# All steps of an attention and feed-forward kernel in another order: what moves when the first V chunk is loaded early and small clears and copies change engine

## The chip, the cores and the metric

The kernel runs on one core of a Trainium2 chip. The metric is the device time of the program in microseconds (us), as the median of timed runs. In the names of the profile PE is the matrix engine (TensorE) and PEld its weight load, DVE is VectorE, ACT is ScalarE, POOL is GpSimd, and SP is the engine that only issues transfers; POOL issues the loads that convert 32 bit floats to 16 bit on the way.

## The reference

Windowed attention (8 global keys, 96 local ones, a bias that falls with distance) and a SwiGLU block behind it. All is given as 32 bit floats.

```python
# q, k, v: (4, 8, 768, 64); w_gate, w_val: (512, 1536); w_out: (1536, 512)
scores = q @ k.transpose(0, 1, 3, 2) / sqrt(64)
keep   = is_global | is_local            # key < 8, or 0 <= query - key < 96
scores = where(keep, scores - slope[h] * dist, -1e9)
a      = softmax(scores, axis=-1)
x      = (a @ v).transpose(0, 2, 1, 3).reshape(3072, 512)
out    = (silu(x @ w_gate) * (x @ w_val)) @ w_out     # (3072, 512)
```

## The kernel before

**Tiles.** A batch of the attention has 768 tokens in two halves of 384. Keys stand in 7 chunks of 120, each with the 8 global keys copied in front, so that a chunk fills 128 rows. Heads go in pairs (0 to 3), pairs in two groups g (0: pairs 0 and 1; 1: pairs 2 and 3). The feed-forward block takes the tokens in 8 tiles t of 384: tile 2b + half is one half of batch b. All weights are kept on chip in 16 bit; the products write to 8 banks of the accumulator memory, which are dealt out in the order of the steps: a product that needs a bank waits until the instruction that read the bank's last contents has run.

**The order.** There is no loop over batches. The string ORDER lists 1035 steps, and the loop at L772 to L774 calls one function for each. Each engine runs its instructions in the order in which the steps issue them and waits only for data, buffers and banks. So ORDER is five queues in one: PE, VectorE, ACT, POOL (mostly loads) and SP (transposes by DMA, stores, small loads). A step that waits holds up all that stands behind it on its engine.

The steps that the text names, with their numbers as arguments:

| step | what it does | engine | line |
|---|---|---|---|
| Lf, Li, Ld | first rows of batch 0; identity; masks' distances (Ld.S.2 is the early mask) | SP, ACT, POOL | L280, L267, L274, L276 |
| Lh.i.half.h0.h1 | half of batch 0's keys (i = 0) or queries (i = 1), four heads | POOL | L284 |
| Lv.b.c | chunk c of batch b's V | POOL | L292 |
| Lw, Lo | parts of gate and value weights (256 KB); thirds of the output weights (512 KB) | POOL | L351, L356 |
| L4, Lr.b.i.h | rows of four heads of batch 1; rows of one head (96 KB) | POOL | L333, L344 |
| Z.b.engine | clears the unused rows of batch b's V buffer, two memsets | by the letter | L309 |
| G.b.c0.c1.engine | copies the 8 global V rows to chunks c0 to c1 - 1 | by the letter | L303, L305 |
| X.b.r...engine | copies V across to the other half of the rows (vX) | by the letter | L319 |
| cast, T, k, q | casts, transposes and places batch 0's keys and queries; k also copies the global keys, always on VectorE (L436) | A or V, PE | L400, L417, L430, L446 |
| b, C, E, V | batch 0's first half: bias, scores, exponentials, weighting of V | PE, ACT | L549, L564, L573, L586 |
| U, kw, qw | batch 1, pairs 0 and 1: transposes on PE, placing | PE, A or V | L455, L463, L473 |
| D.b.pair.i, K.b.pair | the other pairs and batches: transposes by DMA from the rows that Lr loaded; K places keys | SP, VectorE | L483, L490 |
| c, x, m, B | scores, exponentials, masks (M makes them), bias | PE, ACT, VectorE | L520, L530, L539, L504 |
| w, i, j, r, p, W | sums, their inverses, copies beside, spreading, weighting of V (W), scaling (p) | PE, VectorE, ACT | L630, L647, L659, L663, L614, L678 |
| g, t, s, v, h | gate product, tanh, silu, value product, hidden, for tile t and one of 12 columns f | PE, ACT, VectorE | L693, L699, L703, L709 |
| o.t.i.part, e | output product, a quarter each; scaling and store | PE, ACT, SP | L734, L752 |

**Buffers.** V of a batch (vS, tag "vS") has two buffers, dealt in the order of the steps that first use them. Batch 0 and batch 1 take them first. In the order before, batch 3 (Z.3) takes batch 0's and batch 2 (Z.2) takes batch 1's. The staged rows of a batch (stage, tags "kst" and "qst") have two buffers each in the same way. The eight loads that POOL has in flight have one semaphore each, so that the ninth waits for the first to land.

**The order around the change.** The first FFN product is g.0.0; ahead of it stand batch 0's first half and the scores of its second half. From then on PE has FFN products of earlier tiles to do while a batch is prepared. The first product of batch 1 is g.2.1, behind the scaling of its first half (p.1.1.0.1).

Of the kernel before, what the change touches and what calls it, by code (L numbers as in the profile page):

```python
# [84 lines left out]
Z.3.P s.1.10 U.0.1 U.1.1 U.0.0 t.1.0 s.1.0 t.1.1 g.1.11 kw.1.V kw.0.A v.1.10 v.1.1 qw.0.A Lv.1.6
qw.1.A g.1.2 g.1.8 g.1.3 t.1.11 s.1.1 s.1.11 t.1.8 v.1.0 t.1.3 t.1.2 h.1.10 h.1.1 M.1.0 s.1.3 v.1.2
g.0.6 h.1.0 v.1.11 s.1.8 g.1.9 s.1.2 Lv.1.1 M.0.0 g.1.6 h.1.2 Lw.1.1.1 h.1.3 t.1.9 g.0.5 s.1.9
Lr.2.1.3 h.1.11 c.1.0.0.0 t.0.6 t.0.5 t.1.6 s.0.6 c.1.0.0.1 x.1.0.0.1 D.1.2.1 v.1.8 Lv.1.5 g.1.4
s.1.6 g.0.7 g.0.4 h.1.8 s.0.5 v.1.9 v.0.6 Lr.2.0.4 Lv.1.0 t.0.7 x.1.0.0.0 s.0.7 M.3.0 h.1.9 K.1.3
Lo.0 Lo.1 g.1.7 t.0.4 v.1.6 c.1.0.1.0 h.0.6 t.1.7 s.0.4 s.1.7 v.0.7 Lo.2 Lr.2.0.0 h.1.6 v.1.4 Lv.1.2  # L90
h.0.7 v.1.7 t.1.4 g.1.5 v.0.4 Lv.1.4 s.1.4 v.0.5 Lv.1.3 h.1.7 t.1.5 v.1.5 K.1.2 h.1.4 h.0.4 Lr.2.0.3
h.0.5 c.1.1.1.1 Lr.2.1.2 c.1.1.0.0 x.1.0.1.0 c.1.1.0.1 s.1.5 h.1.5 M.2.1 o.0.1.0 o.0.2.0 x.1.1.1.1
x.1.1.0.1 o.0.0.0 Lr.2.0.7 M.2.0 m.1.1.1.1.V o.1.2.0 Lr.2.1.5 Lr.2.1.4 G.1.1.7.S Lr.3.1.2 o.0.0.1
m.1.0.0.0.V Lr.2.0.6 o.1.2.1 x.1.1.0.0 c.1.0.1.1 c.1.1.1.0 o.0.2.1 o.0.0.2 x.1.1.1.0 o.0.1.1 o.1.2.2
o.1.2.3 m.1.1.0.1.V o.0.2.2 m.1.1.0.0.V x.1.0.1.1 m.1.0.0.1.V m.1.1.1.0.V m.1.0.1.1.V m.1.0.1.0.V
w.1.0 X.1.1.0.7.V w.1.1 o.0.1.2 X.1.0.0.7.A i.1.0 i.1.1 o.0.0.3 j.1.0.A r.1.0.0.1 o.0.1.3 W.1.0.1
# [713 lines left out]
```

## Time and profile before

| | before |
|---|---|
| timed runs (us) | 235.59, 237.2, 237.91; median 237.2 |
| span of the profiled execution, first to last instruction (us) | 235.1 |
| time of the profiled execution apart from its span | not given; its DMA packets end at 233.7 us |
| PE busy | 228.1 us, 97% |
| DVE busy | 166.8 us, 71% |
| ACT busy | 117.0 us, 50% |
| POOL busy | 79.1 us, 34%, up to 116 us |
| granted TensorE clock | 1.000 |
| loads and stores | 25.97 MB, 110 GB/s over the span |

How to read it: the profile is of one execution. Times in it are us from the span's start. A busy PE is not a PE at its peak, since its products are pipelined and their ends are modelled. Brackets behind an instruction of the timeline give the engine's idle time ahead of it and what ended it. The view of windows gives for each engine the busy time in a stretch, with the instructions in brackets, then the clock, the DMA share and GB/s.

### The profile page before, as it was taken

What the parts mean: (1) busy time and instruction counts of PE and PEld (TensorE: products, weight loads), DVE (VectorE), ACT (ScalarE), POOL (GpSimd) and SP (SyncE); (2) the same over time, 40 slices, a digit from 0 to 9 for tenths busy, and PEclk for the clock granted to TensorE, in tenths of its full rate; (3) what the DMA queues carried; (4) which work ended last, traced back from release to release, by engine and by line L of the source; (5) the groups of instructions that cost most, each with busy time, mean ns of one, the idle gap of its engine ahead of it and who ended that gap; (6) DMA issues with size and microseconds to landing.
All of it is one profiled execution on the core that took longest, in us unless ns stands there. A gap on an engine that the chain in (4) does not pass through costs nothing.

```text
span 235.1 us, 6093 instructions
## 1 busy us (share of the span) xinstructions
PE 228.1 (97%) x2504; PEld 132.2 (56%) x2504; DVE 166.8 (71%) x385; ACT 117.0 (50%) x220; POOL 79.1 (34%) x113
## 2 busy tenths in 40 slices
PE   7889999998899999999999999999999999999997
PEld 5556556555455656655555565556655565554444
DVE  2698996888549798877798998979776467461020
ACT  4679736783546703827826687744231334140421
POOL 8985778664264079787700000000000000000000
DMA  6999999999999999999999610200000120000323
GB/s 170 190 179 205 203 189 185 130 137 146 202 149 163 204 163 136 110 144 138 146 179 197 68 47 3 89 3 0 3 0 0 45 92 1 0 25 22 134 91 134
DMA packets 88324, 25.97 MB, mean 110 GB/s; under 512 B 78048, under 2 KB 85256, under 8 KB 88296
## 3 DMA queue, kind: packets, MB, share of 16 engines
q0 software_dynamic: 67120, 14.25, 78.7%
q1 hardware_dynamic: 20488, 10.74, 24.5%
q10 hardware_dynamic: 688, 0.59, 0.7%
q8 instruction: 19, 0.31, 0.6%
q14 instruction: 9, 0.07, 0.1%
HBM read 28.93 MB, written 6.29 MB: 150 GB/s over the span
## 4 chain that ended last, share of the span: by engine, by line
PE 65%; DMA 23%; POOL 6%; DVE 3%; issue 1%; ACT 0%; SPq 0%; DVEq 0%; POOLq 0%; ACTq 0%
PE banks L693 39%; PE banks L734 20%; DMA vS<-in_v_dram 6%; DMA kst<-in_k_dram 5%; DMA wv<-in_moe_w_val_dram 4%; DMA qst<-in_q_dram 4%; DMA k<-in_k_dram 3%; PE banks L614 2%; PE banks L520 2%; POOL vS L292 1%; DMA out_dram<-osb 1%; PE banks L723 1%; POOL qst L344 1%; POOL q L284 1%; PE banks L630 1%
## 5 line engine op out<-in xcount | busy, mean ns | idle before, releaser
L699 ACT ACTIVATE th<-banks 128x384 f32<-128x384 f32 x96 | 43.9, 493 | 68.1 <-PE banks L693 66.5
L693 PE MATMUL banks<-xT,wv 128*128 128x384 f16 x384 | 71.7, 326 | 0.4 <-DMA wv<-in_moe_w_val_dram 0.3
L693 PE MATMUL banks<-xT,wg 128*128 128x384 f16 x384 | 70.6, 326 | 0.0
L709 DVE TENSOR_TENSOR hT<-banks,sl 128x384 f16<-128x384 f32 x96 | 50.9, 551 | 22.8 <-PE banks L693 19.8
L734 PE MATMUL banks<-wo,hT 128*128 128x512 f16 x276 | 65.3, 379 | 0.6 <-DMA wo<-in_moe_w_out_dram 0.6
L703 DVE SCALAR_TENSOR_TENSOR sl<-th,banks 128x384 f32<-128x384 f32 x96 | 50.2, 546 | 19.3 <-ACT th L699 18.8
L693 PEld LDWEIGHTS <-wv 128*128 128x128 f16 x384 | 36.8, 98 | 26.3 <-DMA wv<-in_moe_w_val_dram 0.7
L693 PEld LDWEIGHTS <-wg 128*128 128x128 f16 x384 | 37.2, 98 | 25.5 <-DVE xT L678 0.2
L734 PEld LDWEIGHTS <-hT 128*128 128x128 f16 x276 | 26.3, 98 | 29.2 <-DMA wo<-in_moe_w_out_dram 0.8
L530 ACT ACTIVATE at<-banks 128x1008 f16<-128x1008 f32 (+3 forms) x28 | 25.7, 957 | 10.6 <-PE banks L520 9.6
L292 POOL DMA_DIRECT2D vS<-in_v_dram x28 | 25.1, 906 | 5.9 <-DMA qst<-in_q_dram 3.0
L752 ACT ACTIVATE osb<-banks 128x512 f32<-128x512 f32 x23 | 13.5, 597 | 20.0 <-PE banks L734 16.5
L539 DVE TENSOR_TENSOR at<-at,masks 128x1008 f16<-128x1008 f16 (+3 forms) x26 | 16.2, 645 | 5.3 <-ACT at L530 4.9
L344 POOL DMA_DIRECT2D qst<-in_q_dram x20 | 16.8, 843 | 8.4 <-DMA wo<-in_moe_w_out_dram 5.2
L344 POOL DMA_DIRECT2D kst<-in_k_dram x20 | 16.7, 839 | 5.5 <-DMA wo<-in_moe_w_out_dram 2.0
L663 DVE STREAM_TRANSPOSE rb<-dR 128x384 f32<-128x384 f32 x32 | 17.1, 555 | 0.1
L678 DVE TENSOR_TENSOR xT<-banks,rb 128x384 f16<-128x384 f32 x22 | 11.0, 542 | 1.0 <-PE banks L614 0.8
L319 ACT COPY vX<-vS 64x1792 f16<-64x1792 f16 (+2 forms) x7 | 9.0, 1287 | 3.3 <-DMA vS<-in_v_dram 3.1
L520 PEld LDWEIGHTS <-kT 64*64 64x64 f16 x456 | 7.4, 107 | 5.5 <-issue 5.1
L520 PE MATMUL banks<-qT,kT 64*64 64x152 f16 (+9 forms) x456 | 9.1, 214 | 0.9 <-DMA qT<-qst 0.7
L614 PE MATMUL banks<-at,vS 64*64 64x152 f16 (+9 forms) x228 | 8.0, 213 | 0.4 <-DVE hT L709 0.4
L614 PEld LDWEIGHTS <-vS 64*64 64x64 f16 x228 | 6.7, 107 | 2.4 <-issue 2.4
(77 smaller groups left out, 150.6 us busy)
## 6 DMA issues: line engine op xcount, KB each, us to landing
out_dram<-osb SPq DMA_DIRECT2D x23, 256.0 KB, 2.5
vS<-in_v_dram POOLq DMA_DIRECT2D x24, 120.0 KB, 8.4
kst<-in_k_dram POOLq DMA_DIRECT2D x20, 96.0 KB, 7.5
qst<-in_q_dram POOLq DMA_DIRECT2D x20, 96.0 KB, 7.2
wg<-in_moe_w_gate_dram POOLq DMA_DIRECT2D x6, 256.0 KB, 8.1
wv<-in_moe_w_val_dram POOLq DMA_DIRECT2D x6, 256.0 KB, 8.4
wo<-in_moe_w_out_dram POOLq DMA_DIRECT2D x3, 512.0 KB, 13.5
k<-in_k_dram POOLq DMA_DIRECT2D x3, 192.0 KB, 6.0
```

What stands on the lines that cost most here:

```text
L292: nc.gpsimd.dma_start(out=v_of(b)[r0:r0 + n, c, heads(g), :], in_=v[b, heads(g), KC * c:KC * c + n, :].rearrange("h p d -> p h d"))
L344: nc.gpsimd.dma_start(out=rows_of(i, b, h // 2)[:, :, h % 2, :], in_=KQ[i][b, h].rearrange("(t p) d -> p t d", p=128))
L520: nc.tensor.matmul(sc[64 * r:64 * r + 64, hi, col:col + n], lhsT=kTs[2 * g + r][d, k0:k0 + 64], rhs=qTs[b, 2 * g + r][d, q0:q0 + n], start ...
L530: nc.scalar.activation(out=at[:, :, 0:w], in_=sc[:, :, 0:w], func=AF.Exp, scale=scale)
L539: ENG[e].tensor_mul(a2, a2, masks[:, 2 * g:2 * g + 2, x:x + w])
L614: nc.tensor.matmul(num[64 * hi:64 * hi + 64, r, q0 - HB * half:q0 - HB * half + n], lhsT=vSs[b][k, c, h] if up == r else crossed[b][k, c, ...
L663: nc.vector.transpose(rb.rearrange("p (n i) -> p n i", i=32), rbs[b, half][:, g, r].unsqueeze(2).broadcast_to([128, TB // 32, 32]))
L693: nc.tensor.matmul(gv[t, f, which][:, 0:TB], lhsT=w[:, c, 128 * f:128 * f + 128], rhs=xTs[t][:, c, :], start=(c == 0), stop=(c == NC - 1))
L699: nc.scalar.activation(out=th, in_=gv[t, f, 0][:, 0:TB], func=AF.Tanh, scale=0.5)
L703: nc.vector.scalar_tensor_tensor(out=sl, in0=gv[t, f, "t"], scalar=1.0, in1=gv[t, f, 0][:, 0:TB], op0=AluOp.add, op1=AluOp.mult)
L709: nc.vector.tensor_mul(hTs[t][:, f, :], gv[t, f, 1][:, 0:TB], gv[t, f, "s"])
L734: nc.tensor.matmul(ops_t[t, i], lhsT=hTs[t][:, f, 128 * i:128 * i + 128], rhs=wo[:, f, :], start=(f == 0), stop=(f == NFF - 1))
```

## The change

Only the string ORDER changes. It has 1035 steps before and after, and all matmuls, activations and loads are the same ones, but for 19 steps that go to another engine (one of them a copy that was a DMA):

- to VectorE: the clears Z.1 and Z.2 (from POOL), the copy G.0.4.7 (from SP, where it was a DMA), k.1.1, qw.0, X.1.0, and the copies j.1.1, j.2.0, j.2.1, j.3.0 (from ACT);
- to ACT: cast.0.1, cast.1.0, q.1.1, q.3.1, k.2.1, k.3.0, X.1.1, X.2.1; cast.1.1 goes from ACT to VectorE.

The queues change as follows.

- **SP at the start:** Ld.S.2, Lf.S.0.1, Li, Lf.S.0.0 instead of Lf.S.0.1, Li, Ld.S.2, Lf.S.0.0.
- **POOL at the start:** Z.0, kz, Lh.0.0.4.8, Lh.1.0.4.8, Lh.0.1.4.8, **Lv.0.0**, Lh.1.1.0.4, Lh.0.1.0.4, Lv.0.1, Ld.P.1, Lh.1.1.4.8, Lv.0.3, Lv.0.2. Before: Z.0, Z.1, kz, Lh.0.0.4.8, Ld.P.1, Lh.1.0.4.8, Lh.1.1.4.8, Lv.0.0, Lh.0.1.0.4, Lh.1.1.0.4, Lh.0.1.4.8, Lv.0.3, Lv.0.1, Lv.0.2.
- **POOL in the middle:** ... Lr.1.1.6, Lr.1.1.7, Lw.1.1.0, **Lv.2.6**, Lo.0, Lo.1, Lv.1.0, Lo.2, Lv.1.4, Lr.2.0.5, Lv.1.3, Lv.1.6, Lv.1.2, Lv.1.1, Lv.1.5. Before: ... Lr.2.1.3, Lv.1.5, Lr.2.0.4, Lv.1.0, Lo.0, Lo.1, Lo.2, Lr.2.0.0, Lv.1.2, Lv.1.4, Lv.1.3. Lr.3.1.7, of batch 3, is now loaded ahead of batch 1's pair 3.
- **V's buffers:** batch 2 takes batch 0's, cleared by VectorE (Z.2 behind K.1.3), and batch 3 takes batch 1's, cleared by POOL.
- **PE:** the output products begin with o.1.0.0 and not with o.0.1.0; one part of o.0.1 comes behind g.2.4, now the first product of batch 1; the last products are those of tile 7, as before.

The diff, cut to the start and to the steps around Z.2, Lv.2.6 and Lo.0:

```diff
 ORDER = """
-pre Z.0.P Lf.A.1.1 Lf.S.0.1 fill.5 Z.1.P Lf.A.1.0 kz.P Li cast.0.1.V cast.1.0.V cast.1.1.A fill.10
-sl.1 Lh.0.0.4.8 sl.2 Ld.P.1 sl.0 T.1.0.0 T.1.0.1 Ld.S.2 sl.3 T.0.0.1 k.1.0.A sl.4 q.1.0.A q.0.0.V
-b.1.1 Lf.S.0.0 Lh.1.0.4.8 sl.5 sl.7 cast.0.0.V b.1.0 Lh.1.1.4.8 C.1.1 Lv.0.0 C.1.0 E.1.1 Lh.0.1.0.4
-T.0.0.0 b.2.1 b.0.0 E.1.0 k.0.0.V sl.6 b.0.1 T.2.0.0 T.3.0.0 C.0.1 k.2.0.V k.3.0.V Lh.1.1.0.4
-Lh.0.1.4.8 C.0.0 Lv.0.3 Lv.0.1 T.3.0.1 Lv.0.2 E.0.1 T.2.0.1 E.0.0 q.2.0.V G.0.4.7.S pk b.3.0
...
-s.1.6 g.0.7 g.0.4 h.1.8 s.0.5 v.1.9 v.0.6 Lr.2.0.4 Lv.1.0 t.0.7 x.1.0.0.0 s.0.7 M.3.0 h.1.9 K.1.3
-Lo.0 Lo.1 g.1.7 t.0.4 v.1.6 c.1.0.1.0 h.0.6 t.1.7 s.0.4 s.1.7 v.0.7 Lo.2 Lr.2.0.0 h.1.6 v.1.4 Lv.1.2
...
+Ld.S.2 Z.0.P kz.P Lf.S.0.1 Lf.A.1.1 Lf.A.1.0 pre Li fill.5 cast.0.1.A Lf.S.0.0 cast.1.1.V sl.3
+fill.10 sl.2 cast.0.0.V T.1.0.0 T.1.0.1 Lh.0.0.4.8 Lh.1.0.4.8 cast.1.0.A b.1.1 pk sl.6 k.1.0.A
+Lh.0.1.4.8 T.0.0.1 sl.1 Lv.0.0 Lh.1.1.0.4 T.0.0.0 b.1.0 q.1.0.A C.1.0 sl.0 C.1.1 k.0.0.V sl.7
+T.2.0.0 q.0.0.V E.1.1 sl.5 T.3.0.0 E.1.0 Lh.0.1.0.4 Lv.0.1 b.0.0 C.0.0 sl.4 b.0.1 C.0.1 T.2.0.1
+k.2.0.V E.0.0 Ld.P.1 T.3.0.1 Lh.1.1.4.8 E.0.1 b.2.1 T.2.1.0 q.2.0.V C.2.1 G.0.4.7.V w.0.0.0 q.3.0.A
+k.3.0.A b.3.1 C.3.1 b.2.0 Z.1.V k.2.1.A C.2.0 i.0.0.0 E.3.1 Lv.0.3 E.2.0 T.0.1.1 b.3.0 G.0.1.4.V
...
+K.1.3 Z.2.V x.1.0.0.0 s.0.4 g.1.7 g.1.5 h.1.9 s.1.4 t.1.7 Lv.2.6 v.1.7 t.0.6 v.0.7 v.0.6 h.1.8 v.0.4
+Lo.0 m.1.0.0.0.V M.2.0 Lo.1 h.1.6 Lv.1.0 s.1.7 t.1.5 g.0.5 M.2.1 t.0.5 s.0.6 Lo.2 h.1.7 K.1.2 v.1.4
...
+x.1.1.1.1 s.0.7 h.0.7 o.1.0.0 c.1.1.0.1 c.1.1.0.0 h.0.5 o.1.2.0 x.1.0.1.0 v.1.5 Lv.1.6 m.1.0.1.0.V
...
```

More of the change, by code (lines that the diff above doesn't have):

```diff
@@ new lines @@
+Lv.1.2 o.0.0.0 m.1.0.0.1.V x.1.1.0.0 h.1.5 x.1.1.0.1 c.1.0.1.1 Lv.1.1 c.1.1.1.0 Lv.1.5 m.1.1.1.1.V
+Lr.2.1.6 o.0.2.0 o.1.2.1 m.1.1.0.0.V o.0.0.1 x.1.1.1.0 x.1.0.1.1 Lr.2.1.4 o.1.2.2 m.1.1.1.0.V
+o.1.2.3 m.1.1.0.1.V m.1.0.1.1.V o.0.1.0 o.0.2.1 w.1.0 w.1.1 i.1.0 o.1.0.1 X.1.0.0.7.V j.1.0.A
+o.1.0.2 e.1.2 X.1.1.0.7.A o.0.0.2 i.1.1 Lr.2.0.7 o.0.2.2 o.0.0.3 Lr.2.1.3 o.0.2.3 r.1.1.0.1
+r.1.0.0.0 W.1.0.1 r.1.0.0.1 W.1.0.0 p.1.1.0.1.V Lr.2.0.3 o.0.1.1 r.1.1.0.0 e.0.0 p.1.0.0.1.V
+p.1.0.0.0.V o.1.0.3 e.0.2 o.0.1.2 p.1.1.0.0.V g.2.4 g.2.1 t.2.1 g.2.3 g.2.6 Lr.2.1.5 v.2.6 Lr.2.1.7
@@ new lines @@
+Lv.3.6 p.2.1.0.0.V o.1.1.3 n.2.1.1 v.3.7 Lv.3.1 p.2.0.0.1.V p.2.0.0.0.V v.3.5 j.2.1.V D.3.3.1 e.2.0
+r.2.1.0.1 v.3.3 h.3.5 p.2.1.0.1.V D.3.3.0 h.3.3 v.3.10 K.3.2 v.4.8 g.4.8 g.4.6 Lv.3.5 h.3.7 e.1.1
+D.3.1.0 t.4.8 t.4.6 h.3.10 r.2.1.1.1 s.4.8 g.4.11 g.4.3 h.4.8 K.3.3 s.4.6 t.4.11 o.3.1.0 g.4.1
+r.2.1.1.0 s.4.11 t.4.3 t.4.1 s.4.3 D.3.0.1 c.3.1.0.0 p.2.1.1.1.V c.3.1.1.1 x.3.1.1.1 Lv.3.3
+x.3.1.0.0 D.3.0.0 p.2.1.1.0.V Lr.3.1.2 o.3.1.1 Lv.3.2 X.3.1.0.7.A r.2.0.1.0 K.3.1 v.4.3 v.4.1 h.4.3
+o.3.1.2 c.3.1.0.1 D.3.1.1 c.3.1.1.0 v.4.11 x.3.1.1.0 o.3.1.3 s.4.1 h.4.1 x.3.1.0.1 g.4.10
@@ new lines @@
+m.3.1.1.1.V e.3.1 K.3.0 W.2.1.0 h.4.11 c.3.0.1.0 c.3.0.0.1 t.4.10 r.2.0.1.1 s.4.10 p.2.0.1.1.V v.4.6
+g.4.2 p.2.0.1.0.V x.3.0.0.1 m.3.1.0.0.V v.4.10 x.3.0.1.0 t.4.2 h.4.6 m.3.1.0.1.V h.4.10 g.4.4 t.4.4
+s.4.2 s.4.4 c.3.0.0.0 c.3.0.1.1 g.5.4 v.4.5 x.3.0.0.0 v.4.4 x.3.0.1.1 X.3.0.0.7.A m.3.0.0.0.V g.4.5
+m.3.0.1.0.V g.5.1 g.5.6 v.4.2 m.3.0.1.1.V t.5.4 h.4.4 m.3.1.1.0.V t.4.5 o.3.0.0 o.3.0.1 m.3.0.0.1.V
+o.3.0.2 t.5.6 s.4.5 s.5.4 s.5.6 w.3.0 h.4.2 w.3.1 h.4.5 W.3.0.1 o.3.2.0 i.3.0 o.3.2.1 j.3.0.V
@@ new lines @@
+g.6.10 s.6.6 g.6.0 h.6.6 g.6.4 h.5.9 h.6.7 v.6.10 t.6.4 v.5.11 o.4.0.1 r.3.1.1.1 t.6.10 s.6.10
+h.5.11 s.6.4 v.6.4 v.6.3 s.5.0 r.3.1.1.0 h.5.0 r.3.0.1.0 g.6.1 g.6.8 t.6.1 g.6.3 h.6.4 o.4.1.0 t.6.0
+h.6.10 o.4.1.1 s.6.0 s.6.1 v.6.0 t.6.3 p.3.1.1.1.V v.6.8 s.6.3 h.6.3 p.3.0.1.0.V t.6.8 s.6.8
+r.3.0.1.1 g.6.5 v.6.1 p.3.1.1.0.V g.5.2 t.6.5 t.5.2 o.4.2.0 h.6.0 o.4.2.1 o.4.0.2 o.4.1.2 h.6.1
+p.3.0.1.1.V s.5.2 g.6.2 o.4.2.2 o.4.0.3 o.4.1.3 t.6.2 h.6.8 v.6.2 e.4.0 g.6.9 s.6.2 o.4.2.3 v.5.2
+g.5.8 s.6.5 t.6.9 v.5.8 h.6.2 e.4.1 s.6.9 g.7.5 t.7.5 g.7.8 h.5.2 t.5.8 v.7.5 s.7.5 o.5.2.0 o.5.2.1
@@ L147 @@
+h.7.10 o.7.0.0 o.7.1.1 h.7.9 h.7.6 o.7.1.2 o.7.1.3 e.7.1 o.7.0.1 o.7.0.2 o.7.0.3 o.7.2.0 e.7.0
+o.7.2.1 o.7.2.2 o.7.2.3 fill.2 e.7.3 fill.4 fill.7 e.7.2
 """
```

117 lines of the change are left out of this document (45 added, 72 removed).

## The prediction

> **What bounds the kernel now.** I read the summary of engines first, then DMA's slices, then the busy time of four stretches of my own choosing, and last the chain that ended last.
>
> ```profile
> PE 228.1 (97%) x2504; PEld 132.2 (56%) x2504; DVE 166.8 (71%) x385; ACT 117.0 (50%) x220; POOL 79.1 (34%) x113
> DMA  6999999999999999999999610200000120000323
> 0.00:21.12 21.12, 17.87 (x307) 11.66 (x308) 14.66 (x52) 14.23 (x27) 18.37 (x37) 1.00 1.35 184
> 21.12:75.81 54.69, 52.91 (x668) 30.72 (x658) 43.30 (x96) 33.68 (x62) 32.91 (x42) 1.00 1.83 168
> 75.81:152.00 76.19, 75.82 (x1073) 44.57 (x1071) 65.76 (x152) 44.44 (x82) 27.86 (x34) 1.00 1.41 123
> 152.00:235.10 83.10, 81.46 (x477) 45.30 (x469) 43.11 (x87) 24.69 (x51) 0.00 (x0) 1.00 0.12 42
> ```
>
> The second number of a stretch is its length, the third the busy time of PE, and the clock is 1.00 in all four. Both orders issue the same 2504 matmuls, so only PE's idle time and the start can change. From 75.81 us to 152 us PE lacks 0.37 us, and what it lacks after 152 us lies at the very end (the last products, then the last output). So the whole change is decided before about 84 us: in the 21.12 us before the first FFN product (g.0.0), and in the 1.78 us (54.69 - 52.91) that PE lacks from there to the first product of batch 1 (g.2.1, at 75.81 us). DMA is at 9 in every slice from the second on, to some 130 us: loads pace that part.
>
> ```profile
> 58.26 0.82 PE L520 MATMUL banks<-qT,kT 64*64 64x160 f16 x44 [0.68 <-DMA qT<-qst]
> 59.71 4.13 PE L734 MATMUL banks<-wo,hT 128*128 128x512 f16 x18 [0.64 <-DMA wo<-in_moe_w_out_dram]
> 75.81 3.41 PE L693 MATMUL banks<-xT,wg 128*128 128x384 f16 x20
> 82.78 0.24 PE L614 MATMUL banks<-at,vS 64*64 64x128 f16 x2 [0.37 <-DVE hT L709]
> 54.65 14.83 DMA vS<-in_v_dram
> 69.56 0.62 DVE vX L319
> 70.21 0.60 DVE dT L647
> 70.83 0.48 DVE dR L651 x2
> 71.40 0.59 DVE dT L647
> 72.40 1.43 DVE L663 STREAM_TRANSPOSE rb<-dR 128x384 f32<-128x384 f32 x3
> 73.75 0.98 DVE L678 TENSOR_TENSOR xT<-banks,rb 128x384 f16<-128x384 f32 x2
> ```
>
> The first four rows are of PE's timeline (start, length; in brackets the idle time and its releaser), the next five of the chain, the last two of VectorE's timeline. The last chunk of batch 1's V is issued at 54.65 us and lands 14.83 us later, at 69.48 us; VectorE, which had stood, at once copies it across (X), inverts two denominators (dT and dR, twice), spreads and scales, and g.2.1 starts at 75.81 us, 6.33 us behind the landing. That landing is the bound that the middle has to beat.
>
> **The start.** The new order puts the early mask ahead of Lf.S.0.1 and Li on SP, Z.1 on VectorE, and the casts of heads 2 and 3 one behind the other on ACT. The rows are of the engines' timelines; `POOL vS L292` is of the chain, and the row with 120.0 KB of the loads with their time to landing.
>
> ```profile
> 4.52 0.53 PE L417 MATMUL banks<-ident,k 128*64 128x128 f16 x6
> 0.73 1.41 POOL L309 MEMSET vS<- 32x256 uint32 x4 [0.29 <-POOLq L791]
> 6.70 0.35 DVE L400 CAST k<-k 128x384 f16<-128x384 f32 x1
> 6.87 1.23 ACT L573 ACTIVATE at<-banks 128x336 f16<-128x336 f32 x2 [0.86 <-PE banks L564]
> 10.31 0.48 ACT L446 COPY qT<-banks 128x384 f16<-128x384 f16 x1
> 5.09 0.54 ACT L430 COPY kT<-banks 128x360 f16<-128x360 f16 x2 [0.32 <-PE banks L417]
> 14.43 0.63 ACT L430 COPY kT<-banks 128x96 f16<-128x96 f16 x3
> 5.86 0.93 POOL vS L292
> vS<-in_v_dram POOLq DMA_DIRECT2D x1, 120.0 KB, 5.9
> 16.14 0.73 PE L597 MATMUL banks<-at,pairs 128*64 128x216 f16 x16 [0.21 <-DVE kT L430]
> 17.11 0.57 DVE L647 STREAM_TRANSPOSE dT<-banks 128x384 f32<-128x384 f32 x1
> 20.19 1.02 DVE L675 TENSOR_TENSOR xT<-banks,rb 128x384 f16<-128x384 f32 x2
> 21.12 2.77 PE L693 MATMUL banks<-xT,wg 128*128 128x384 f16 x16
> ```
>
> Half of the four memsets, 0.7 us, leaves POOL's queue ahead of its first load, so every load of that queue is issued 0.7 us earlier. Against that, the first transposes come some 0.5 us later (4.52 us now), and C.1 waits for the copy of the global keys, which now stands on VectorE behind cast.0.0 (6.70 us now; its data lands late in either order). I put the first exponentials at 7.6 us instead of 6.87 us. From there ACT's own queue sets the pace: two pairs of exponentials (1.23 us each), q.3.0 and k.3.0 (0.48 and 0.54, both ACT's now), k.2.1 (0.63), E.3.1, E.2.0 and E.2.1 (one short and one long make the 1.23, so 0.35, 0.88, 0.35), q.0.1 (0.48) and E.3.0 (0.88): 7.05 us, and 0.3 us of waits for scores by my estimate, so about 14.95 us. Then w.0.0.1 starts at 15.05 us instead of 16.14. VectorE follows with i.0.0.1 (0.95 to its end), three spreads (0.49 each) and four scalings (0.47 each): 4.3 us, one spread more than now, and g.0.0 starts at 20.2 us instead of 21.12: **-0.9 us**, taken from bounds of +0.6 (the half us of the late start stays and nothing is gained) and -1.5. The long copy G.0.4.7 is a wait that is added: VectorE stands there until V's first chunk is in. That chunk is issued at 5.86 us now and lands 5.9 us later; the new order takes a clear (0.7) and a load (0.75) from ahead of it, so it is in by 10.3 us, rather earlier, since less is in flight before it. Behind the copy k.3.0's global keys, Z.1 and i.0.0.0 are queued, and C.3.1 and T.1.1.0 wait for those; in the sum above VectorE arrives at 10.2 us, so the wait is nothing, and each us that the chunk is later costs a us of the start.
>
> ```profile
> 13.20 0.90 DVE L305 COPY vS<-vS 8x1536 f16<-8x1536 f16 x1
> 14.11 0.70 POOL L351 DMA_DIRECT2D wg<-in_moe_w_gate_dram  x1 [0.19 <-issue]
> ```
>
> G.0.4.7 itself costs 0.9 us of VectorE by its twin's row, G.0.1.4, and lies in front of i.0.0.0, off the chain above. During that twin POOL stood 0.19 us and went on 0.01 us after its end. The Trainium skill, "SBUF — State Buffer", section "Who interferes with whom", says that a VectorE copy in a two-port mode and a GpSimd instruction shut each other out for the whole instruction; by that rule the new copy holds POOL's descriptors back by up to its 0.9 us, where the row gives 0.19, and the sum below would be 0.7 us worse. The trace agrees in kind, the row decides the size.
>
> **The middle.** Here POOL's queue counts. Lv.2.6 now stands ahead of the output weights (Lo.0, Lo.1, Lo.2) and of all of batch 1's V, and it waits for Z.2, on VectorE behind K.1.3, which waits for the transpose D.1.3.0.
>
> ```profile
> 37.16 3.75 SPq L483 DMA_TRANSPOSE kN<-kst  x2
> kN<-kst SPq DMA_TRANSPOSE x2, 8.5
> 51.13 0.45 DVE L490 COPY kT<-kN 128x720 f16<-128x720 f16 x1
> 0.86 0.27 DVE L362 MEMSET ones<- 128x256 f16 x1 [0.86 <-PEq L791]
> 48.34 2.25 POOL L356 DMA_DIRECT2D wo<-in_moe_w_out_dram  x3 [1.43 <-DMA qst<-in_q_dram]
> DMA to landing us min/median/max: 11.3/13.5/15.5
> qst<-in_q_dram POOLq DMA_DIRECT2D x1, 96.0 KB, 4.1
> kN<-kst SPq DMA_TRANSPOSE x2, 3.4
> ```
>
> The fourth to sixth of these are a memset on VectorE, POOL's issue of the three wo loads and their time to landing; the seventh is the landing of one load into an empty queue near 84 us, and the second and the eighth are the landing of transposes beside a full queue (37 to 42 us) and beside an empty one (74 to 84 us). D.1.3.0 is issued at 37.16 us now. In the new queue two row loads (96 KB) and two weight loads (256 KB) more lie ahead of its rows, 704 KB, which at the 168 GB/s of that stretch (its last number) are 4.3 us, less the 0.7 us: issued at about 40.5 us, landed 7 to 8.5 us later (its queue is by then no longer refilled), K.1.3 at 47.8 us. Z.2 is two memsets, 0.56 us by the memset row (0.7 us, POOL's price above, is the other end). So POOL stands at Lv.2.6 from about 41 us to 48.9 us (K.1.3 0.5, Z.2 0.56), and Lo.0 is issued near 49.6 us. With nothing ahead of it in its queue it lands some 6 us later (4.1 us and the larger size), 55.8 us, where PE needs it at about the same time. From Lo.0's landing (48.34 + 11.3 = 59.64 us) to the last V chunk's, 9.8 us pass now, with two wo, three V and a row load; the new order has three full V chunks and a small one more there, 408 KB or 2.5 us: 12.3 us, so the last V chunk is in at about 68.1 us. A count of the whole queue gives 68.5 us (69.48, less 0.7 for the start, less 0.2 for the mix) if the engines never run dry. I take **69.0 us**, with 67.2 and 71.9 us as ends.
>
> Behind it X, i.1.1, four spreads and four scalings stand as now, but i.1.0 (0.60 and 0.48 us, 1.1 with the gap) is done ahead of X. So the first product of batch 1 (now g.2.4) starts at 75.81 - 0.5 - 1.1 = 74.2 us. PE alone could be there at 75.81 - 0.9 - 1.7 - 0.65 = 72.6 us (the start; the waits of the middle; one part of o.0.1, which now comes after), so V and VectorE set it, and the 0.9 us of the start, the waits for transpose and Lo.0 (0.68 and 0.64) and a possible stall of 1 us behind K.1.3 all lie under it. That part of o.0.1 is owed: +0.65. The wait of W.1.1 (0.37 at 82.78 us) goes, since its banks are now given back by earlier steps: -0.4. Sum: -0.5 - 1.1 + 0.65 - 0.4 = **-1.35 us**.
>
> The engine moves after that (j from ACT to VectorE; X of batch 2 to ACT; Z.3 on POOL in place of Z.2) stand beside a PE that lacks 0.37 us in 76 us: nothing, and 0.5 us either way if that cover is thin. The tail has the same last products: nothing.
>
> **The rivals.** *Fast*: the transposes find POOL's queue empty and take 3.4 us, not 8.5. Then K.1.3 goes when VectorE gets there (46.5 us), V is in at 67.2 us, and PE itself is the bound at 72.6 us: -3.2 + 0.65 - 0.4 = -3.0 us. For it: the 3.4 us; against: the queue is still full when they are issued. *Slow*: K.1.3 stays where it is now, at 51.13 us, because the rows of pair 3 or the transposes come late. POOL then stands at Lv.2.6 3.3 us longer with Lo.0 and all of batch 1's V behind it, DMA runs dry, V is in at 71.9 us: +2.4 - 1.1 + 0.65 - 0.4 = +1.6 us, and 1 us more for each us that K.1.3 is later still. It decides from K.1.3 at about 49.7 us. *Nothing*: the start gains nothing, V lands at 70 us or a new small wait takes the rest: 0 us.
>
> **How the numbers follow.** The profile has a span of 235.1 us, and the runs 235.59 to 237.91, median 237.2; the sum is made against the span and carried to the median: 237.2 - 1.35 = 235.9 us. Forecast (-0.5 to -2.3 us) 0.42, fast 0.24, slow 0.20, nothing 0.14. One per cent, 2.4 us, is about what a measurement can tell from no change. Fast lies past it for the most, with the forecast's edge: 0.32. Of slow, what is later than 52 us, with unforeseen waits: 0.15. The rest, 0.53, is within. The range reaches from fast with another 1 us (232.9) to slow with another 0.6 us (239.4).
>
> **What would show it.** The first FFN product at 20.2 us; POOL's gap ahead of Lv.2.6, ended by VectorE's memset near 48.9 us; the last V chunk of batch 1 near 69 us with VectorE's X right behind it; g.2.4 near 74.2 us; no wait at W.1.1; PE unbroken from there. It is wrong if K.1.3 is far from 47.8 us, if the DMA engines stand idle near 50 us, or if PE waits after 84 us.

## The result, and the profile after

The changed kernel takes 238.04 us in the median of 20 runs (236.54 to 240.59), the kernel before 236.59 us in 20 runs beside them: ratio 1.0063, 95% interval 1.0040 to 1.0087. It is 1.5 us slower. The ratio leaves out one of the 20 runs after, which is over 1.5% above the fastest. The profiled execution has a span of 236.0 us, 0.9 us over that of before.

The summary of engines, the slices of clock and DMA, and the windows of the kernel after (columns as before: length, busy time of PE, its weight loads, VectorE, ACT and POOL, then clock, DMA share, GB/s; the last window lies inside the first):

```profile
PE 230.0 (97%) x2504; PEld 132.6 (56%) x2504; DVE 168.9 (72%) x401; ACT 116.8 (50%) x209; POOL 78.2 (33%) x109
...
PEclk9799999999999999999999999999999999999999
DMA  7999999979999999999997710110000021110133
```
```profile
0.00:21.97 21.97, 18.93 (x307) 11.97 (x308) 13.86 (x49) 14.64 (x31) 18.80 (x36) 0.92 1.37 188
21.97:75.18 53.21, 52.66 (x665) 30.43 (x655) 44.06 (x100) 34.14 (x59) 32.78 (x41) 1.00 1.65 167
75.18:152.00 76.82, 76.11 (x979) 43.89 (x978) 66.87 (x166) 41.95 (x65) 26.57 (x33) 1.00 1.38 121
152.00:236.00 84.00, 82.30 (x566) 46.30 (x565) 44.14 (x89) 26.11 (x55) 0.00 (x0) 1.00 0.12 43
8.00:11.00 3.00, 3.00 (x28) 1.40 (x28) 2.23 (x13) 1.23 (x2) 3.00 (x4) 0.50 1.80 177
```

Three things differ from before. A row for PE's clock is there, which the page of before did not need: the granted clock is 0.50 from 8 to 11 us, and the first FFN product comes at 21.97 us (21.12 before). From there to the first product of batch 1 PE lacks 0.55 us instead of 1.78, and DMA has a slice of 7 where it ran dry, near 50 us. And from 75 to 152 us PE now lacks 0.71 us instead of 0.37. So the start loses 0.85 us, PE stands some 1.2 us less in the middle, and the stretch behind it loses again. In lengths: the start is 0.85 us longer, g.0.0 to the first product of batch 1 is 1.48 us shorter (53.21 against 54.69), and the rest is 1.53 us longer (160.82 against 159.29; one part of o.0.1, 0.65 us, has moved into it). That is the 0.9 us of the spans.

```profile
5.10 0.36 PE L417 MATMUL banks<-ident,k 128*64 128x128 f16 x6 [0.55 <-ACT k L400]
7.28 0.36 PE L417 MATMUL banks<-ident,k 128*64 128x128 f16 x6 [1.01 <-DVE k L400]
9.61 0.90 PE L554 MATMUL banks<-early,slopeI 128*128 128x432 f16 x2
49.83 0.65 POOL L292 DMA_DIRECT2D vS<-in_v_dram  x1 [9.81 <-DVE sl L703]
47.90 0.34 DVE L490 COPY kT<-kN 128x720 f16<-128x720 f16 x1
48.52 0.64 DVE L309 MEMSET vS<- 32x256 uint32 x2
70.01 0.82 DVE L319 COPY vX<-vS 64x1792 f16<-64x1792 f16 x1 [1.94 <-issue]
120.75 0.25 PE L614 MATMUL banks<-at,vS 64*64 64x152 f16 x2 [0.42 <-DVE sl L703]
124.87 0.81 PE L693 MATMUL banks<-xT,wv 128*128 128x384 f16 x4 [0.17 <-DVE hT L709]
```

These rows are of the timelines of PE, POOL and VectorE. The first three are the start: PE stands 0.55 and 1.01 us for casts, then its bias products take 0.90 us where they took 0.53 before:

```profile
7.59 0.53 PE L554 MATMUL banks<-early,slopeI 128*128 128x432 f16 x2
```

The next four are the middle: POOL stands 9.81 us at Lv.2.6 until K.1.3 (47.90) and the clear Z.2 (48.52) have run (the releaser named is the step behind Z.2), and X, which goes when the last V chunk is in, starts at 70.01 us. The last two are waits that before did not have: PE stands for a bank that VectorE gives back. By the starts of PE's steps, against the same steps in a run without these waits (e9, below), they cost 0.59 us ahead of W.2.0.0, 0.33 us ahead of v.4.8, and 0.28 us at g.4.8 behind it: 1.2 us. The expectations below put the first at 0.49 us and the sum at 1.1.

### The profile page after: what moved, and what is told of

The parts are those of the page before. It is cut to its first block, busy times and chain, and to the rows that moved or that the text cites. A ratio compares the mean times of both kernels' runs of the same rounds, so it can differ in the third digit from the quotient of the medians.

```text
span 236.0 us, 6083 instructions
## 1 busy us (share of the span) xinstructions
PE 230.0 (97%) x2504; PEld 132.6 (56%) x2504; DVE 168.9 (72%) x401; ACT 116.8 (50%) x209; POOL 78.2 (33%) x109
## 4 chain that ended last, share of the span: by engine, by line
PE 89%; DVE 5%; DMA 2%; ACT 2%; issue 1%; SPq 1%
PE banks L693 52%; PE banks L734 23%; PE banks L520 3%; PE banks L614 2%; DMA k<-in_k_dram 2%; PE banks L630 1%; DVE xT L678 1%; DVE rb L663 1%; PE banks L417 1%; PE banks L723 1%; PE banks L554 1%; PE banks L564 1%; DVE dT L647 1%; PE banks L455 1%; PE banks L394 1%
## 5 line engine op out<-in xcount | busy, mean ns | idle before, releaser
L699 ACT ACTIVATE th<-banks 128x384 f32<-128x384 f32 x96 | 45.0, 493 | 75.3 <-PE banks L693 73.2
L693 PE MATMUL banks<-xT,wg 128*128 128x384 f16 x384 | 72.2, 326 | 0.6 <-DVE xT L678 0.4
L734 PE MATMUL banks<-wo,hT 128*128 128x512 f16 x276 | 67.0, 379 | 0.0
L539 DVE TENSOR_TENSOR at<-at,masks 128x976 f16<-128x976 f16 (+3 forms) x26 | 15.6, 642 | 1.4 <-ACT at L530 1.4
L319 ACT COPY vX<-vS 64x1792 f16<-64x1792 f16 (+2 forms) x8 | 10.7, 1336 | 0.7 <-issue 0.6
L647 DVE STREAM_TRANSPOSE dT<-banks 128x384 f32<-128x384 f32 x9 | 5.1, 568 | 5.1 <-PE banks L630 4.5
```

Source lines behind the costliest of these rows:

```text
L539: ENG[e].tensor_mul(a2, a2, masks[:, 2 * g:2 * g + 2, x:x + w])
L693: nc.tensor.matmul(gv[t, f, which][:, 0:TB], lhsT=w[:, c, 128 * f:128 * f + 128], rhs=xTs[t][:, c, :], start=(c == 0), stop=(c == NC - 1))
L699: nc.scalar.activation(out=th, in_=gv[t, f, 0][:, 0:TB], func=AF.Tanh, scale=0.5)
L734: nc.tensor.matmul(ops_t[t, i], lhsT=hTs[t][:, f, 128 * i:128 * i + 128], rhs=wo[:, f, :], start=(f == 0), stop=(f == NFF - 1))
```

## The experiments

The theory from the traces ("Theory A"): the start loses by PE's slow products, and VectorE's late banks at 119 to 126 us eat what the middle gives. All ratios are to the kernel before on the same chip, with 95% intervals.

**The fills: PE kept busy at the start (e4).**

```diff
-fill.10 ... T.0.0.1 sl.1 Lv.0.0 Lh.1.1.0.4 T.0.0.0
+fill.12 ... T.0.0.1 sl.1 Lv.0.0 Lh.1.1.0.4 warm.4 T.0.0.0     # warm.4: four more fill products
```

> The kernel after, with six more fill products (256 columns, some 0.22 us each) on PE: two ahead of the first transpose and four ahead of T.0.0.0, where PE stands 0.55 and 1.01 us before its clock falls to 0.50 from 8 to 11 us. Rival C (the clock is the start's loss): no run shows a clock of 0.993, g.0.0 comes at 20.9 to 21.2 us, and 0.8 to 1.0 us come back: ratio to before 1.002 to 1.003. Theory A puts less on it: only 6 of 20 runs of the kernel after have the lower clock, their spans have a median of 236.75 us against 236.05 for the other 14, so 0.7 us in 3 runs of 10: 0.2 us in the middle run, ratio 1.005 to 1.006, while the clock does stay at 1.000.

Measured: 1.0014 (0.9985 to 1.0043), g.0.0 at 20.69 us, clock 1.00 in all 12 runs. So it is rival C's size: by the two ratios some 1.2 us come back, not the 0.2 us that A put on it. A had counted only the runs with a granted clock under 1; the next experiments show why that was too few.

**The early mask back in third place on SP (e8).**

```diff
-Ld.S.2 ... Lf.S.0.1 ... Li
+Lf.S.0.1 ... Li Ld.S.2
```

> The kernel after with one step moved: the early mask (Ld.S.2) is third on SP's queue again, behind Lf.S.0.1 and Li, as in the kernel before; no fills. Theory A (PE's idle stretches at 4.55 to 5.10 and 6.27 to 7.28 us let its rate fall in most runs): the first transpose comes 0.4 us earlier (4.7 us), the data for cast.0.0 no earlier (Lf.S.0.0 stays fourth), so the second stretch stays at 1 us or more and the slow matmuls stay: g.0.0 21.5 to 22 us, ratio 1.004 to 1.007. Rival B (the order of SP's loads makes the late start): g.0.0 at 21.0 us or before, ratio 1.001 to 1.003.

Measured: 1.0132 (1.0096 to 1.0169), g.0.0 at 22.45 us. Rival B falls: the order of SP's loads is not the loss. PE's timeline shows the first transpose at 4.39 us, and what the mask then costs:

```profile
6.07 0.32 PE L549 MATMUL banks<-early,slopeI 128*128 128x144 f16 x4 [0.89 <-DMA early<-early_c]
...
7.64 0.53 PE L417 MATMUL banks<-ident,k 128*64 128x128 f16 x6 [0.95 <-DVE k L400]
8.10 0.90 PE L554 MATMUL banks<-early,slopeI 128*128 128x432 f16 x2
```

PE stands for the mask now, then again for the cast, and is slow afterwards. It is slower than the changed kernel by 0.7%, more than A expected; in its profile a wait of 0.96 us at 107 us is added to the start. The traces of f3 and f4 have the same wait, 0.52 and 0.83 us. There PE stands ahead of c.2.0.1.0 for the transpose of batch 2's queries (D.2.0.1), which in all three lands 0.13 to 0.14 us before that product starts. In the order before it landed some 5 us ahead of its product, in the kernel after 0.5 us: a cover that the new order made thin, and that failed in 3 of the 13 profiled executions with the new order behind the start.

**The start after with the rest before (e2).** The order after up to i.0.1, then all other steps in the order before.

> The other half of the pair: the order of the kernel after up to the first inverses of tile 0's second half (i.0.1, some 25 us), then all other steps in the order of the kernel before. Theory A: the later start (0.85 us) is all that is left: ratio to before 1.002 to 1.004, g.0.0 near 22 us, no wait of PE over 0.2 us between 119 and 126 us. Rival S (all is lost at the start): ratio 1.006. Rival R (the start is covered by the middle, where loads pace the work): ratio 1.000, with the first product of batch 1 no later than 75.8 us.

Measured: 1.0013 (0.9992 to 1.0033). PE's timeline and two windows of e2:

```profile
5.49 0.53 PE L417 MATMUL banks<-ident,k 128*64 128x128 f16 x6 [0.92 <-ACT k L400]
...
7.71 0.90 PE L554 MATMUL banks<-early,slopeI 128*128 128x432 f16 x2
...
75.94 0.81 PE L693 MATMUL banks<-xT,wg 128*128 128x384 f16 x4
```
```profile
8.00:11.00 3.00, 3.00 (x31) 1.42 (x30) 2.20 (x12) 1.25 (x3) 3.00 (x4) 1.00 1.81 178
119.00:127.00 8.00, 8.00 (x133) 5.02 (x132) 7.08 (x20) 4.03 (x10) 0.00 (x0) 1.00 0.97 173
```

Here the products are slow (0.53 for a transpose, 0.90 for a bias product) under a recorded clock of 1.00, from the first transpose on: a slow start need not show in the clock's row, and the lengths of equal products tell it. g.0.0 comes at 21.93 us, 0.8 us late, and yet the first product of batch 1 comes at 75.94 us (75.81 before). In the old order the loads cover a late start; by this product rival R is right for that order; the ratio alone doesn't part it from A's 1.002.

**Before, with less fill (e10).** The same test from the other side.

```diff
-cast.1.1.A fill.10
+cast.1.1.A fill.2
```

> The kernel before with eight of its fill products taken out ahead of the first transpose (2 instead of 10), so that PE stands idle from 2.8 to 4.5 us. Theory A: PE's products are then slow for 3 us or more somewhere between 4.5 and 11 us (transposes of 0.53 us, bias products of 0.9 us), g.0.0 comes at 21.6 to 22.3 us instead of 21.12, but here the loads cover it, since POOL waits for nothing on VectorE in the middle: the first product of batch 1 (g.2.1) stays within 0.3 us of 75.81 us, ratio 1.000 to 1.002. Rival P (a late start is paid in full in this order too): g.2.1 at 76.4 us or later, ratio 1.003 to 1.005. Rival N (PE's rate doesn't depend on its idle time): g.0.0 at 21.1 us.

Measured: 1.0003 (0.9975 to 1.0030). PE's timeline:

```profile
6.13 0.88 PE L554 MATMUL banks<-early,slopeI 128*128 128x432 f16 x2
...
21.69 0.99 PE L693 MATMUL banks<-xT,wg 128*128 128x384 f16 x5
...
75.69 1.14 PE L693 MATMUL banks<-xT,wg 128*128 128x384 f16 x6
```

The products stay slow some 2 us longer than before, g.0.0 is 0.57 us late, and nothing of it arrives at 75.7 us. As theory A had it.

**Lv.2.6 moved off its place (e7).** With the fills, and Lv.2.6 behind the last V chunk of batch 1, so that POOL waits for nothing on VectorE.

```diff
-Z.2.V x.1.0.0.0 s.0.4 g.1.7 g.1.5 h.1.9 s.1.4 t.1.7 Lv.2.6 v.1.7
+Z.2.V x.1.0.0.0 s.0.4 g.1.7 g.1.5 h.1.9 s.1.4 t.1.7 v.1.7
...
-c.1.1.1.0 Lv.1.5
+c.1.1.1.0 Lv.1.5 Lv.2.6
```

> The kernel after with the six fill products, and Lv.2.6, which waits for VectorE's clear Z.2, moved behind the last V chunk of batch 1 (Lv.1.5) on POOL's queue. In the kernel with fills POOL issues Lv.2.6 at 48.55 us, after K.1.3 (46.62 us) and Z.2, and the last chunk lands at 68.8 us. Theory G (this gate ties batch 1's V to VectorE, so that each us of a late start reaches the V loads): Lo.0 issued before 45 us, no slice of DMA under 9 near 50 us, the last V chunk in by 67 us, the waits of PE at W.1.0.0 and g.2.4 (0.32 and 0.60 us) under 0.2 us, g.2.4 near 73.3 us, 0.5 to 0.9 us less: ratio 0.997 to 1.000. Rival H (the gate is hidden, PE and VectorE set g.2.4 anyway): V earlier but g.2.4 not before 73.9 us, ratio 1.001 to 1.002. Rival W (the loads that now come sooner collide with the transposes D.1.3 and D.1.2): K.1.3 later than 48 us, slower than the kernel with fills.

Measured: 1.0200 (1.0164 to 1.0236): rival W, at a price that it had not put in numbers. The first row is of the kernel after (loads issued from 36 to 44 us: count, median us to landing), the others of e7: the same view, the timelines of VectorE and PE, and windows (its line numbers are 6 higher).

```profile
kN<-kst SPq DMA_TRANSPOSE x2, 5.9
```
```profile
kN<-kst SPq DMA_TRANSPOSE x1, 12.2
```
```profile
52.34 0.35 DVE L496 COPY kT<-kN 128x720 f16<-128x720 f16 x1 [3.19 <-DMA kN<-kst]
54.07 1.65 PE L699 MATMUL banks<-xT,wg 128*128 128x384 f16 x8 [2.26 <-DVE sl L709]
```
```profile
50.00:54.00 4.00, 1.81 (x12) 0.98 (x10) 1.45 (x7) 0.60 (x1) 0.40 (x2) 1.00 1.67 128
54.00:60.00 6.00, 5.93 (x27) 3.15 (x27) 4.50 (x13) 2.99 (x5) 2.07 (x3) 0.72 1.59 170
```

POOL issues the output weights at 39.6 us and the V chunks behind them, and the transposes that K.1.3 needs then take 12.2 us instead of 5.9 to land. VectorE stands 3.19 us at K.1.3, PE 2.26 us behind it, and after that stand PE's clock is low once more (0.72 over the next 6 us). V is in early (the last chunk of batch 1 at 65.8 us) in spite of a late g.0.0 (23.14 us), so without the gate V no longer moves with the start: that half of theory G holds. Its gain does not come, since from g.0.0 to g.2.4 it is 56.17 us here and 53.41 us in e4. In this order POOL's stand of 9.8 us, with DMA dry at its end, keeps the queues clear for the transposes; that it costs nothing is not shown. Nor is the ratio the price of this move alone: the start was slow in spite of the fills, 2.45 us behind e4's (the first cast came at 6.01 us, 1 us later than in e4), and the granted clock was under 1 in 5 of the 6 runs. So the fills make a slow start rarer and don't rule it out.

**The late copies on ACT (e3), and the late part mended whole (e9).** e3 is the first line of each pair, e9 both:

```diff
-j.2.0.V ... j.2.1.V
+j.2.0.A ... j.2.1.A
...
-i.2.0 j.2.0.A r.2.0.0.0 g.3.10 o.2.0.3 W.2.0.1 t.3.10 s.3.10 r.2.1.0.0
+i.2.0 g.3.10 o.2.0.3 W.2.0.1 t.3.10 s.3.10 j.2.0.A r.2.0.0.0 r.2.1.0.0
```

> The kernel after, with the copies j.2.0 and j.2.1 (0.72 us each on VectorE, 118.92 and 123.05 us) back on ACT, which is idle there. Theory A: these two copies stand ahead of s.3.10 and of h.3.5, h.3.3, which give back the banks that PE waits for at 120.75, 124.87 and 125.80 us (0.49, 0.33 and 0.28 us): 0.8 to 1.1 us come back, the three waits fall under 0.15 us each, ratio to before 1.002 to 1.003. Rival L (VectorE is late there whatever is on it, since the inverses come late behind w.2.1): the waits move to the next bank and the ratio stays at 1.006.

Measured: 1.0054 (1.0028 to 1.0081). The waits at v.4.8 and g.4.8 are gone, the one ahead of W.2.0.0 stays, at 0.63 us. ACT's timeline says why:

```profile
117.80 0.88 ACT L659 COPY dR<-dR 32x24 f32<-32x24 f32 x4 [0.75 <-DVE dR L651]
118.71 0.49 ACT L699 ACTIVATE th<-banks 128x384 f32<-128x384 f32 x1
```

On ACT the copy j.2.0 stands ahead of t.3.10, for which s.3.10 and so the bank wait: the copy left one queue and came in front of the same bank on another.

> The kernel after with the late part alone mended: j.2.0 and j.2.1 on ACT, t.3.10 and s.3.10 ahead of j.2.0 and r.2.0.0.0; no fills at the start. With both edits the three waits of PE at 119 to 126 us were gone and the ratio was 0.9965; with the fills alone it was 1.0014. Theory A (the two losses add): the waits are gone here too, the start stays as in the kernel after, and 1.0 to 1.2 us come back: ratio 1.001 to 1.002. Rival D (the banks are late only because the fills put PE ahead): nothing comes back, ratio 1.005 to 1.007.

Measured: 0.9976 (0.9939 to 1.0014), all three waits gone. Step for step, PE gets back 0.59, 0.33 and 0.28 us of the kernel after there. Rival D falls. The ratio is lower than A's 1.001 to 1.002; its interval reaches to 1.0014.

**Both edits (e5).**

> The kernel after with the six fill products at the start, j.2.0 and j.2.1 on ACT, and s.3.10 ahead of j.2.0 and of the first spread (r.2.0.0.0) on their queues. With j.2.0 on ACT alone, t.3.10 stood behind it (118.71 us) and the wait ahead of W.2.0.0 stayed at 0.63 us; here t.3.10 goes first. Theory A (the loss is PE's slow matmuls between 7.5 and 11 us, 1.1 us, and VectorE's late banks at 119 to 126 us, 1.1 us, and they add): g.0.0 at 20.7 us, all three waits under 0.2 us, W.3.0.0 1.1 us ahead of the kernel with fills alone (151.92 us), ratio to before 0.996 to 0.998. Rival D (PE ahead of VectorE only meets the next late bank): W.3.0.0 at 151.4 to 152.0 us, ratio 1.000 to 1.002.

Measured: 0.9965 (0.9936 to 0.9995). Theory A, with g.0.0 at 20.91 us, W.3.0.0 at 150.95 us (151.92 with the fills alone), and no wait over 0.2 us in the stretch. This version beats both kernels.

**The two by two on one chip (f1 to f4).** What was open: the four ratios came from three chips and did not add up.

> The kernel after, unchanged, on the same chip as the three that follow. From its first 20 runs: ratio 1.004 to 1.009, the granted clock under 1 in about 3 runs of 10.

> The kernel after with the six fills. By the traces the slow products cost 1.1 us where they occur. If the two losses are independent: 0.5 to 1.2 us under f1, ratio 1.001 to 1.004. If the start is nothing by itself: as f1.

> The kernel after with the late part mended (j on ACT, t.3.10 and s.3.10 first). The waits of PE in the trace of after sum to 1.1 us there. If independent: 1.0 to 1.3 us under f1, ratio 1.001 to 1.003. If the late banks cost more than PE's waits show (the first run gave 2 us): ratio 0.996 to 0.999.

> Both edits. If they add: 1.8 to 2.4 us under f1, ratio 0.996 to 0.999, and 0.5 to 1.2 us under f3. If the fills are needless once the late part is mended: as f3, within 0.2%.

| | waits at 119 to 126 us as changed | mended |
|---|---|---|
| start as changed | f1 1.0039 (1.0000 to 1.0079) | f3 1.0012 (0.9979 to 1.0045) |
| with fills | f2 1.0011 (0.9985 to 1.0037) | f4 0.9973 (0.9944 to 1.0002) |

The fills give 0.28 and 0.39%, the late part 0.27 and 0.38%, some 0.6 to 0.9 us each, and together 0.66%: they add, as far as the intervals tell. A single step of the table is no larger than an interval; the corners f1 and f4 only touch at their ends, and the first comparisons of the same two kernels (1.0063, from 1.0040; 0.9965, to 0.9995) stand apart. The granted clock was under 1 in 18 of the 68 runs of after, e3, e9, f1 and f3, which have the changed start and no fills, and in none of the 48 of e4, e5, f2 and f4, which have them. But it was under 1 in 27 of 104 runs of the kernel before beside the experiments too, and those took 237.59 us in the median, against 236.46 us where it was 1.00. So a low clock is no mark of the changed order. That the changed order pays for a late start rests on the traces (e2 and e10 against f1 and after); where the clock fell in those runs of before is not kept, and the kernel before was not run with fills.

**The start before with the rest after (e1, e6).** e1 is the order before up to g.0.0, then the order after; e6 the same with the banks of the rest dealt from a list.

> Steps ahead of the first FFN product (g.0.0) stand as in the kernel before, all others in the order of the kernel after. Theory A (the traces): the kernel after loses 0.85 us before g.0.0 (21.97 against 21.12 us), gains some 1.2 us by the middle, and loses some 1.2 us in three new waits of PE between 119 and 126 us. By A the 0.85 us come back at most: 0.6 to 0.9 us under the kernel after, ratio to before 1.002 to 1.004, g.0.0 at 21.1 us, the three waits still there. Rival S (all is lost at the start): faster than before by what the middle gives, ratio 0.995 to 0.999. Rival R (the start is covered, since V's last chunk sets the first product of batch 1): ratio stays at 1.006.

Measured: 1.0180 (1.0137 to 1.0224), outside of all three. The start dealt the banks in another phase, so that steps 160 and 190 us later got banks that come late:

```profile
15.95 0.36 PE L417 MATMUL banks<-ident,k 128*64 128x128 f16 x6 [1.05 <-DMA k<-in_k_dram]
...
182.85 0.32 PE L693 MATMUL banks<-xT,wg 128*128 128x384 f16 x1 [0.78 <-DVE sl L703]
...
215.81 0.81 PE L693 MATMUL banks<-xT,wv 128*128 128x384 f16 x4 [0.98 <-DVE sl L703]
```

> The start of the kernel before and the rest of the kernel after once more, with the banks of the rest dealt as in the kernel after (its numbers 0, 1 and 2, 3 exchanged). The first such pair dealt other banks late, and PE stood 0.95 us at 182 us and 1.15 us at 215 us. Theory A: those two waits and the 0.4 us at 152 us are gone, about 2.5 us less than that pair's 240.8 us: 238.0 to 238.5 us, ratio 1.005 to 1.008 if g.0.0 stays at 21.9 us as there, 1.002 to 1.004 if it comes at 21.1 us. Rival S (the late steps cost nothing, all comes from the start): ratio 0.997 to 1.000.

Measured: 1.0086 (1.0052 to 1.0119), 238.43 us: the two late waits are gone and the time is the one that A gave for a late g.0.0 (21.55 us), which comes late since this start waits for key rows (1.05 us in e1, first row). So the old start is no better with the new rest, and rival S fell: not all of the loss is at the start.

## Why the prediction was wrong

The forecast was 235.9 us, 1.35 us under before; it came out some 1.5 us over. The time lies inside the stated range only because that reached to 239.4 us for rival Slow, which did not occur: that is luck. The middle, which the prediction took for the core, came near the times worked out. The terms on both sides of it failed, and two errors make up the difference: g.2.4 came 0.98 us behind the predicted 74.2, since the late start was not covered, and the waits of PE at 119 to 126 us cost 1.2 us. -1.35 + 0.98 + 1.2 is +0.83 us, against +0.9 in the profiled spans. In f1, where PE started at full rate, g.2.4 came 0.64 us early, and the same sum gives -0.79 us, against -0.7 (234.4 against 235.1). Neither error alone turns the sign. The medians lie another half us apart; what makes that up is not shown.

**The start (-0.9 us) was near for PE at full rate, and that condition was not in the sum.** f1 is the same kernel in an execution with bias products of 0.53 us:

```profile
8.56 0.53 PE L554 MATMUL banks<-early,slopeI 128*128 128x432 f16 x2
20.36 0.66 PE L693 MATMUL banks<-xT,wg 128*128 128x384 f16 x3
48.22 0.65 POOL L292 DMA_DIRECT2D vS<-in_v_dram  x1 [8.61 <-DVE sl L703]
68.42 0.79 DVE L319 COPY vX<-vS 64x1792 f16<-64x1792 f16 x1 [1.98 <-issue]
73.56 2.90 PE L693 MATMUL banks<-xT,wg 128*128 128x384 f16 x16 [0.37 <-DVE xT L678]
```

g.0.0 at 20.36 us stands against 20.2 predicted; in e3, which has the same start, it comes at 20.86 us, also with bias products of 0.53 us. Where they take 0.90 us (after, e2, e9, f3) it comes at 21.86 to 22.10 us. The prediction had read "the clock is 1.00 in all four" off the stretches of before and carried it over to a start in which PE waits for casts; the term is +0.85 us in the profiled execution. The stands alone do not decide it: e3 stood 0.67 and 0.94 us for its casts, much as after did, and kept the full rate; f1 stood 1.24 us once and then ran at the full rate, f3 1.19 us and did not. The Trainium skill, "TensorE: Matmul & The Clock Gate", Part 1, tells of a clock that is halved until PE has been busy for a window of about 3.4 us, the window running free, so that one kernel can find it in different phases; the 0.50 over 3 us, and 0.53 and 0.90 us for the same product of one kernel, agree. By its figure an idle window as long is needed to fall back; here PE never stood more than 1.01 us at a time between its first product and the fall at 8 us, so the measurement differs, unless, as Part 4 of that page has it, transposes don't count as busy; no run here tells that apart.

**"All lie under it" failed; with the waits below it turned the sign.** The prediction had the start covered by V's landing. From g.0.0 to g.2.4 it is 53.20 us in f1 and 53.21 us in after (73.56 - 20.36 and 75.18 - 21.97): the start is paid in full. In all twelve profiles with the new order behind the start and the gate in it, this stretch is 52.7 to 53.8 us, for starts from 20.36 to 22.45 us. The reason is the gate that the change puts in: Lv.2.6 waits for Z.2, which stands in VectorE's queue behind FFN steps, so the loads of V move with the start (X at 68.42 and 70.01 us). With the old rest, whose POOL waits for nothing on VectorE there, the same late start was covered (e2, e10); with the gate moved away, V came early behind a late start (e7).

**The middle came out in its times, but not for the reason given.** Lo.0 was issued at 50.47 us (49.6 predicted), the last V chunk was in by 69.93 us (69.0) and g.2.4 came at 75.18 us (74.2), all late by the start; in f1 it is 48.87, 68.34 and 73.56. The wait of W.1.1 is gone as said. K.1.3 met its number by luck, at 47.90 us against 47.8: the sum had it wait for transposes of 7 to 8.5 us, but they took 5.9 us and had landed at 46.23 us, and it waited for VectorE's own queue, which was late by the start. In f1 it came at 46.30 us, which is the condition of rival Fast (46.5 us, when VectorE gets there), though not with that rival's transposes of 3.4 us. The rival Slow did not occur; e7 shows its first step, late transposes and K.1.3 at 52.34 us.

**"Nothing" after 84 us was the third error.** The term was mis-sized: 0 with 0.5 either way, measured 1.2 us of waits in the trace, and 0.6 to 0.9 us by the two by two, whose mended executions (f3, f4) also show the wait at 107 us. The prediction saw that j moved to VectorE beside a PE that lacks only 0.37 us, but did not ask which bank stands behind the copy. VectorE's timeline after, and the windows of after and f4:

```profile
118.92 0.73 DVE L659 COPY dR<-dR 32x24 f32<-32x24 f32 x4
...
120.18 0.52 DVE L703 SCALAR_TENSOR_TENSOR sl<-th,banks 128x384 f32<-128x384 f32 x1
...
123.05 0.72 DVE L659 COPY dR<-dR 32x24 f32<-32x24 f32 x4
```
```profile
119.00:127.00 8.00, 7.29 (x125) 4.42 (x124) 7.81 (x24) 2.46 (x5) 0.00 (x0) 1.00 0.84 142
```
```profile
119.00:127.00 8.00, 8.00 (x132) 4.94 (x130) 7.61 (x20) 4.59 (x14) 0.00 (x0) 1.00 0.97 152
```

j.2.0 (118.92) and a spread run ahead of s.3.10 (120.18), whose bank W.2.0.0 needs, and j.2.1 (123.05) ahead of the h steps that v.4.8 and g.4.8 wait for. VectorE is busy for 7.81 of 8 us there, where a mean of 66.87 in 76.82 looks roomy; ACT has 2.46. In f4 PE is unbroken.

**The rule on VectorE and POOL** that was weighed made no difference: G.0.4.7 ran from 12.36 us for 0.93 us, and POOL, which stood 0.47 us, went on at 13.07 us, inside the copy:

```profile
12.36 0.93 DVE L305 COPY vS<-vS 8x1536 f16<-8x1536 f16 x1
13.07 0.72 POOL L351 DMA_DIRECT2D wv<-in_moe_w_val_dram  x1 [0.47 <-DMA k<-in_k_dram]
```

**A slip without effect.** The lower end of the range, 232.9 us, is 0.3 us below what it is said to be made of (237.2 - 3.0 - 1.0 = 233.2).

## What to carry to other kernels

Where a change lets a load wait for a compute engine, ask what that engine is late by: a delay that was covered by free-running loads is then paid in full. A small step that goes to another queue costs nothing only if no bank, buffer or activation that the busiest engine is about to need stands behind it there: read that from the window where it lands, not from the engine's mean. And where an early stretch of short products gets gaps, compare the lengths of equal products with those of before; a few spare products in the gaps kept the recorded clock up in the 48 runs of e4, e5, f2 and f4, but only in 1 of the 6 of e7, where the start came later still and PE stood again at 52 us.

## What was not expected of the hardware

The same bias products took 0.53 or 0.90 us in the same kernel from one execution to the next, and a slow stretch was recorded as a clock of 0.50 (after, 8 to 11 us) or as 1.00 (e2, the same stretch). Stands of PE of nearly the same length were followed by either (e3 and after, f1 and f3). A stand of PE of 2.26 us was followed by a clock of 0.72 over 6 us (e7). A transpose by DMA landed in 5.9 us while POOL's queue was drained, and in 12.2 us beside a full one.
